# Output scatters through disjoint views, token splits one slot apart, and a reordered first joint in an attention, expert and dense kernel

## Chip, cores and metric

The kernel runs on one core of a Trainium2 chip. The metric is the device time of that core in microseconds (us), the median of three runs.

## What is computed

The reference is a chain of three parts. Attention runs over 4 batches, 8 heads, 576 positions and 64 values per head; four heads see a window of 32 positions, four a dilated one (every fourth of 128). Its output is a matrix of 2304 tokens by 512. Then comes a mixture of 8 experts in which each token goes to one expert alone, and last a dense layer over all tokens:

```python
e_idx = argmax(x @ w_gate + modality_bias[modality_id])
for e in range(8):                       
    out[e_idx == e] = gate_w * (relu(x[e_idx == e] @ w1[e]) @ w2[e])
...
h = x @ w_in                             
g = where(h >= 1, h, where(h <= -1, 0, (h + 1) ** 2 / 4))
return g @ w_out
```

The expert layers are 512 to 1024 to 512, the dense ones 512 to 2048 to 512. All of it is fp32 with the accuracy kept by splitting each operand into a high part and a low part (the rest) in a rounded format: a product is three matmuls, high by high, low by high and high by low.

## The kernel before

The engines are TensorE (PE, whose weight loads are shown as PEld), VectorE (DVE), ScalarE (ACT), GpSimd (POOL) and SyncE (SP, which issues most transfers). Each engine works off its instructions in the order in which the program records them, since the scheduling is manual; an engine that waits holds up all that is queued behind it. So the order of the calls in the code is the order on each engine.

**Attention and routing** come first. The attention output is gated and written to memory, and the routing (class `Route`) counts on DVE which token goes where; its results are registers that the engines load from a tile `ri` (`load_regs`, L570, through `values`, L560).

**The experts** run as steps 0 to 15, each a chunk of 256 tokens of one expert. `gather` (L592) collects the token rows by indirect DMA on POOL, in two halves of 128; `scale` (L620, DVE) or `scale_act` (L616, ACT) multiplies them by the gate; `tx` (L627) transposes them on PE into a bank and splits them into `xh` (ACT) and `xl` (DVE). `half_a` (L777) runs the first expert layer, eight output tiles `fb` of `l1_wide`; `half_b` (L803) the second, four output tiles `d` of `l2_wide`. Between the tiles stand pieces of other work: `work` yields parts of the weight conversion; `small_x`, `small_1`, `small_h`, `small_2`, `small_y`, `small_out` handle a remainder of up to 32 tokens and stand under a branch on the register `sm` (L667); `resplit` (L885) splits an expert's weights again, under a branch on the register `c` (L887); `load_w` under one on `ld`. Step 0 and step 1 overlap with the routing and are special: `first` (L733) is step 0's second half, `small_ids` and the register loads stand in step 1's `half_a`, and `positions` behind it computes where each token lies. Steps 9 to 15 stand under nested branches on the number of chunks that the routing counted; for this input they are not taken, though the rows for step 9 are gathered, scaled and transposed in steps 6 to 8, as the rows of any next step.

**The dense part** (`dense`, L1340) takes the tokens in three groups g of 768 and the 2048 hidden columns in eight pairs of blocks, so 24 pairs n. A pair's first product is a 2x2 block product in the manner of Strassen, with seven products instead of eight: the seven slots j of a pair (`SLOTS`, L1480). A slot's matmuls go to bank X or Y, and `part` keeps three of the partial products (copies on ACT, L1501) until `joined` (L1413, DVE) adds them. Each finished block goes through `relu` (ACT: relu and square, L1395 and L1396), `square` (DVE: the clamp of L1403, then ACT's cast to the high part, L1404) and, a slot later, `lows` (DVE: the low part, L1411). The second product (`l2_tile`, L1422) sums six banks po[0] to po[5] over the eight pairs of a group; `flow` puts one or two of its tiles into each slot, always those of the pair before. The first pair has no seven products but four plain blocks, in banks po[5], po[4], po[3] and Y (L1464).

Two further streams of work stand in the slots. The tokens of the next group are summed (`y_sum`, raw sums T1 to T4) and split (`y_split`, L1371): a cast to the high part on ACT, and right behind it the low part on DVE; the list `late` says in which slot. And the weights of the next pair are split (`split_in`, `split_out`, one piece per `next`) in the first eight pairs, after which they come back from a cache in memory. When the last pair of a group has finished a bank, `send` (L1430) copies it on ACT and scatters its 128 rows of 512 values to the output by an indirect DMA on POOL (L1435), 18 in all, six per group. All 18 write the same tensor `out`, and each waits for the one before.

## Time and profile before

| | |
|---|---|
| runs | 802.9, 804.3, 804.7 us |
| median of the runs | 804.32 us |
| the profiled execution's own time | 804.42 us |
| its span in the profile | 802.5 us |
| TensorE busy | 746.1 us, 93% of the span |
| weight loads / DVE / ACT / POOL busy | 661.5 / 506.7 / 379.3 / 98.5 us |
| mean granted clock of TensorE, full being 1 | 0.982 |

How to read it: the span runs from the first to the last instruction of one profiled execution, and all times in it count from the span's start. An engine that is busy for most of the span is not thereby the bound of every stretch, so the table of stretches shows busy time and the granted clock for windows of 25 us. The list of waits names, for an engine and a line, what its last semaphore came from, with the total in us, how many times and the longest. In the timeline a row in square brackets shows how long its engine had stood idle and what ended that. "ACTq" or "PEq" is the engine's sequencer, which also does register loads and branches.

### The profile page before, as it was taken

The page shows a single profiled execution, that of the slowest core. Times are in us where ns is not written, and L with a number is a line of the kernel's source. Part 1 is how long each engine was busy: PE and PEld are TensorE (multiplying, and loading weights), DVE is VectorE, ACT ScalarE, POOL GpSimd, SP SyncE. Part 2 cuts the span into 40 slices and gives each one's busy share as a digit, 9 for nine tenths or more (in the row PEclk, how much of TensorE's full clock was granted, in tenths as well). Part 3 has the DMA queues.
Part 4 walks back from the last instruction along what each step waited for, and adds up shares of the span by engine and source line. Part 5 has one row for each costly group of instructions (what it writes and reads, how often), then busy time and mean ns, then how long its engine had stood idle before and what let it go on. Part 6 is the DMA issues. An engine that isn't in the chain of part 4 may idle for free. (4 is left out here: it accounts for less than half of the span.)

```text
span 802.5 us, 15304 instructions
## 1 busy us (share of the span) xinstructions
PE 746.1 (93%) x5545; PEld 661.5 (82%) x5547; DVE 506.7 (63%) x1217; ACT 379.3 (47%) x948; POOL 98.5 (12%) x101
## 2 busy tenths in 40 slices
PE   7998879789999999999879999899999999999991
PEld 4887769788998999889868898788889878889980
DVE  4789886684677888784677777754454454433430
ACT  3667643213323323532457666675354566444550
POOL 3335542120100001000000000001000002000002
PEclk9999989999999999999999999999999999999996
DMA  7779751277989968713429766387446435653411
GB/s 196 205 224 288 237 166 42 55 245 242 327 274 318 339 185 269 271 59 105 125 103 339 290 250 223 151 295 278 156 170 229 178 145 205 257 193 145 146 64 65
DMA packets 66345, 161.55 MB, mean 201 GB/s; under 512 B 8448, under 2 KB 25856, under 8 KB 60240
## 3 DMA queue, kind: packets, MB, share of 16 engines
q1 hardware_dynamic: 62592, 148.58, 54.5%
q0 software_dynamic: 3520, 11.55, 4.3%
q8 instruction: 48, 0.79, 0.4%
q14 instruction: 41, 0.34, 0.1%
q10 hardware_dynamic: 144, 0.29, 0.1%
HBM read 119.36 MB, written 41.04 MB: 200 GB/s over the span
## 5 line engine op out<-in xcount | busy, mean ns | idle before, releaser
L1403 DVE SCALAR_TENSOR_TENSOR t<-x,t 128x384 f32<-128x384 f32 x92 | 51.3, 558 | 76.7 <-ACT t L1396 76.6
L1426 PE MATMUL d_o<-d_ob,gh 128*128 128x512 f32 x288 | 90.5, 395 | 0.0
L1426 PE MATMUL d_o<-d_plain,gh 128*128 128x512 f32 x288 | 89.6, 392 | 0.0
L643 PE MATMUL ps_e<-hh,whi 128*128 128x256 f32 x288 | 82.7, 287 | 0.4
L643 PE MATMUL ps_e<-hl,whi 128*128 128x256 f32 x288 | 81.1, 282 | 0.0
L643 PE MATMUL ps_e<-hh,wlo 128*128 128x256 f32 x288 | 81.0, 281 | 0.0
L1395 ACT ACTIVATE t<-x 128x384 f32<-128x384 f32 x92 | 48.3, 525 | 54.2 <-DVE x L1416 54.2
L1404 ACT CAST gh<-t 128x384 fp32r<-128x384 f32 x96 | 49.4, 515 | 44.6 <-DVE t L1403 44.3
L1411 DVE TENSOR_TENSOR gl<-t,gh 128x384 fp32r<-128x384 f32 x96 | 53.2, 554 | 17.8 <-ACT gh L1404 15.5
L1176 ACT ACTIVATE p<-ps_s,nb 128x96 f32<-128x96 f32 x144 | 47.1, 346 | 33.2 <-DVE su L1184 32.3
L1426 PEld LDWEIGHTS d_o<-d_ob,gh 128*128 128x128 f32 x288 | 53.4, 190 | 5.8
L1426 PEld LDWEIGHTS d_o<-d_plain,gh 128*128 128x128 f32 x288 | 53.0, 188 | 6.1
L1426 PE MATMUL d_o<-d_ob,gl 128*128 128x512 f32 x144 | 57.4, 399 | 0.0
L1426 PE MATMUL d_o<-d_plain,gl 128*128 128x512 f32 x144 | 57.1, 396 | 0.0
L1416 DVE TENSOR_TENSOR x<-d_y,d_u 128x384 f32<-128x384 f32 x46 | 25.5, 554 | 48.7 <-ACT d_u L1501 48.7
L643 PEld LDWEIGHTS ps_e<-hh,whi 128*128 128x128 f32 x288 | 54.5, 189 | 1.0 <-issue 1.0
L643 PEld LDWEIGHTS ps_e<-hh,wlo 128*128 128x128 f32 x288 | 54.5, 189 | 0.0
L643 PEld LDWEIGHTS ps_e<-hl,whi 128*128 128x128 f32 x288 | 54.4, 189 | 0.0
L1396 ACT ACTIVATE t<-t 128x384 f32<-128x384 f32 x96 | 50.5, 526 | 3.0
L1501 ACT COPY d_u<-d_x 128x384 f32<-128x384 f32 x46 | 22.0, 478 | 61.7 <-PE d_x L1383 61.7
L1435 POOL DMA_INDIRECT out<-o,pid x18 | 17.6, 975 | 267.5 <-ACT o L1434 198.1
L643 PE MATMUL ps_s<-xh,whi 128*128 128x256 f32 x152 | 45.6, 300 | 5.0 <-DVE hl L654 3.2
(439 smaller groups left out, 1902.9 us busy)
## 6 DMA issues: line engine op xcount, KB each, us to landing
raw<-in_w SPq DMA_DIRECT2D x48, 512.0 KB
d_ab<-cache SPq DMA_DIRECT2D x15, 1024.0 KB
d_ab<-cache SPq DMA_DIRECT2D x15, 768.0 KB
r<-in_w_in SPq DMA_DIRECT2D x16, 512.0 KB
r<-in_w_out SPq DMA_DIRECT2D x16, 512.0 KB
wsc<-cva SPq DMA_DIRECT2D x32, 256.0 KB
cache<-d_ab SPq DMA_DIRECT2D x8, 1024.0 KB
d_ob<-cache SPq DMA_DIRECT2D x8, 1024.0 KB
```

The costliest lines, as they stand in the source:

```text
L643: self.tc.nc.tensor.matmul(ps, a, b, start=(i == 0 and j == 0), stop=(i == n - 1 and j == 2))
L1176: nc.scalar.activation(p[:, j, :], s[:, j, :], ACTF.Exp, scale=scale, bias=nb[:, j:j + 1], accum_out=su[:, j:j + 1])
L1395: nc.scalar.activation(b.t, x, ACTF.Relu, scale=0.5, bias=0.5)
L1396: nc.scalar.activation(b.t, b.t, ACTF.Square)
L1403: nc.vector.scalar_tensor_tensor(b.t, x, 1.0, b.t, op0=ALU.max, op1=ALU.min)
L1404: nc.scalar.copy(b.h, b.t)
L1411: nc.vector.tensor_tensor(b.l, b.t, b.h.bitcast(F32), op=sub)
L1416: nc.vector.tensor_tensor(x, bank, other, op=add)
L1426: nc.tensor.matmul(po[i], a[:, q], o[:, x, f, :], start=(first and j == 0), stop=(last and j == 2))
L1435: nc.gpsimd.indirect_dma_start(out=out[:, :], out_offset=bass.IndirectOffsetOnAxis(ap=pid[:, n:n + 1], axis=0), in_=t, in_offset=None)
L1501: nc.scalar.copy(part[("p1", "u2", "u3")[j // 2]], bank)
```

## The change

It has five parts, all in the order or the place of work; no arithmetic changes.

1. Each scatter writes through its own view of the output, of 18 that are declared disjoint.
2. In step 0's second half, `scale_act(1)` comes ahead of the third tile, and half of the re-split ahead of the fourth; the other half goes into step 1. In step 1 the load of the nine `sm` registers on PE and ACT becomes one of four before the seventh tile of the first layer and one of five before the second tile of the second layer; the small pieces, the routing's `positions` and the transposes for step 2 move later.
3. What steps 7 and 8 did for steps 9, 10 and 11 (scaling, transposes, a gather) stands in the branch of step 9.
4. The first dense pair's blocks go to X, Y, po[5] and po[4], and T2 and T1 are split in its third and fourth block's place.
5. `y_split` is cut into `y_high` (the cast) at the end of a slot and `y_low` (the subtraction) behind the `lows` of the next; the second sums T3 and T4 come a slot earlier, output weights' split a slot later, and `split_in` has one pause more.

```diff
                 late = rt.late_counts()
             next(late)
         for d in range(HP):
+            if d == 2:
+                self.scale_act(1)
             self.l2_wide(d, slice(0, 256))
             if d == 0:
                 rt.late_ids(self.b.A[0])
...
                 rt.more_ids(self.b.A[1])
                 next(regs)
             if d == 2:
-                self.scale_act(1)
                 self.tx(1, 0)
                 self.tx(1, 1)
-        self.resplit(1, 0, 8)
+                self.resplit(1, 0, 4)
         next(regs)
         next(regs)
         return regs
...
                 self.w.load(i, self.regs[s]["ne"])
     def half_a(self, s, wide, work, rt=None):
-        at = {5: self.small_x, 6: self.small_1, 7: self.small_h} if s == 1 else {0: self.small_x, 2: self.small_1, 4: self.small_h}
+        at = {7: self.small_x} if s == 1 else {0: self.small_x, 2: self.small_1, 4: self.small_h}
         for fb in range(8):
             if s == 1 and fb == 2:
                 self.small_ids(rt, work)
             if s == 1 and fb == 6:
                 self.scale(2)
-            if s == 1 and fb == 4:
-                self.load_regs("sm", R_SM, 1, 10, [ENG.PE, ENG.Activation])
+            if s == 1 and fb == 6:
+                self.load_regs("sm", R_SM, 1, 5, [ENG.PE, ENG.Activation])
                 self.scale3(1)
             if s > 1 and fb in (2, 4, 6):
                 self.resplit(s, fb, fb + 2)
...
                 self.small(s, at[fb])
                 if at[fb] == self.small_h:
                     self.sum_h()
+            if s == 1 and fb == 1:
+                self.resplit(1, 4, 8)
             if wide:
                 self.l1_wide(fb)
                 if s > 1 or fb > 1:
                     next(work, None)
                     next(work, None)
-            if fb == (7 if s == 1 else 3):
+            if s > 1 and fb == 3:
                 self.load_w(s, 0, 4)
+        if s == 1:
+            self.small(s, self.small_1)
+            self.load_w(s, 0, 4)
         for _ in work:
             pass
-    def half_b(self, s, wide, work):
-        self.small(s, self.small_2)
-        self.load_w(s, 4, 8)
-        if wide:
-            self.tx(s + 1, 0)
-            self.tx(s + 1, 1)
+    def half_b(self, s, wide, work, rt=None):
+        late = s == 1
         off = bass.ds(self.regs[s]["off"], 256)
         for d in range(HP):
-            if d == 2:
+            if late and d == 1:
+                self.load_regs("sm", R_SM, 5, 10, [ENG.PE, ENG.Activation])
+                self.small(s, self.small_h)
+                self.sum_h()
+                rt.positions()
+            if d == (3 if late else 0):
+                self.small(s, self.small_2)
+                self.load_w(s, 4, 8)
+            if wide and s != 8 and d == (2 if late else 0):
+                self.tx(s + 1, 0)
+                self.tx(s + 1, 1)
+            if not late and d == 2:
                 self.small(s, self.small_y)
                 if s > 0:
                     self.sum_y()
-            if d == 3:
+            if not late and d == 3:
                 self.small(s, self.small_out)
             if wide:
                 self.l2_wide(d, off)
...
             if d == 2:
                 self.scale3(s + 1)
                 self.resplit(s + 1, 0, 2)
+        if late:
+            self.small(s, self.small_y)
+            self.sum_y()
+            self.small(s, self.small_out)
         for _ in work:
             pass
...
             self.load_sp(9, NS)
             self.load_mode(10, NS)
             self.load_off(9, NS)
+            self.scale(9)
+            self.scale(10)
+            self.tx(9, 0)
+            self.tx(9, 1)
+            self.gather(11)
         n = CV_STEPS[s] if cv else (0, 0)
         parts = cv.start(n[0]) if n[0] else []
         self.either(s, lambda wide: self.half_a(s, wide, cv.work(parts, True, s < 7) if cv else self.ahead(s, 0, regs), rt))
...
         self.gather3(s + 1)
         if s == CV_LAST + 1:
             self.m2.load_in()
-        if rt:
-            rt.positions()
         if cv:
             cv.loads()
         more = cv.start(n[1]) if n[1] else []
-        self.either(s, lambda wide: self.half_b(s, wide, cv.work(more, False, s < 7) if cv else self.ahead(s, 1)))
-        self.gather(s + 3)
-        self.scale(s + 2)
+        self.either(s, lambda wide: self.half_b(s, wide, cv.work(more, False, s < 7) if cv else self.ahead(s, 1), rt))
+        if s != 8:
+            self.gather(s + 3)
+        if s not in (7, 8):
+            self.scale(s + 2)
         if cv:
             cv.loads()
...
         V.tensor_tensor(a21, a11, a21, op=ALU.subtract)
         V.tensor_tensor(a11, a22, a11, op=ALU.subtract)
         V.tensor_tensor(a12, a12, a11, op=ALU.subtract)
+        yield
         yield
         x = t.rearrange("p f (a k) -> p (f a) k", a=2)
         S.copy(s[:, 0], x)
...
         tp = st.enter_context(tc.tile_pool(name="d_t", bufs=3))
         ps = st.enter_context(tc.tile_pool(name="d_ps", bufs=1, space=PSUM))
         op = st.enter_context(tc.tile_pool(name="d_out", bufs=6))
+        outs = dram_disjoint_views(out, NT)
         m2.more(yp)
         X, Y = (ps.tile([128, 512], F32, name=f"d_{c}")[:, 0:G2] for c in "xy")
         po = [ps.tile([128, 512], F32, name=f"d_o{i}") for i in range(6)]
...
             for c in range(2):
                 nc.vector.tensor_tensor(raw[k][c], src(g, a, c), raw[b][c] if b in raw else src(g, b, c), op=sub)
-        def y_split(g, k, c, b=None, vec=False):
+        def y_high(g, k, c, b=None, vec=False):
             h, l = yt[k][c]
             b = DIRECT.get(k, b)
             x = raw[k][c] if b is None else src(g, b, c)
             (nc.vector.tensor_copy if vec else nc.scalar.copy)(h, x)
-            nc.vector.tensor_tensor(l, x, h.bitcast(F32), op=sub)
+            y_lows.append((h, l, x))
+
+        def y_low():
+            while y_lows:
+                h, l, x = y_lows.pop(0)
+                nc.vector.tensor_tensor(l, x, h.bitcast(F32), op=sub)
+
+        def y_split(*a, **k):
+            y_high(*a, **k)
+            y_low()
+
+        y_lows = []
         def mm(bank, lst, start, stop):
             n = len(lst)
...
                 t = op.tile([128, 512], F32, tag="o", name="o")
                 nc.scalar.copy(t, p)
                 nc.gpsimd.indirect_dma_start(
-                    out=out[:, :], out_offset=bass.IndirectOffsetOnAxis(ap=pid[:, n:n + 1], axis=0), in_=t, in_offset=None)
+                    out=outs[n][:, :], out_offset=bass.IndirectOffsetOnAxis(ap=pid[:, n:n + 1], axis=0), in_=t, in_offset=None)
         def queue(n, blk):
             m = n % NP
...
         for i, (t, f) in enumerate(((0, 0), (0, 1), (1, 1), (1, 0))):
             k1, k2 = (("B11", "B21"), ("T3", "B22"))[t]
             w = m2.plain[:, :, f, :]
-            bank = (po[5], po[4], po[3], Y)[i][:, 0:G2]
+            bank = (X, Y, po[5], po[4])[i][:, 0:G2]
             mm(bank, [(w, c, yt[k1][c]) for c in range(2)] + [(w, 2 + c, yt[k2][c]) for c in range(2)], True, True)
             if i == 0:
                 for k in ("T3", "B22"):
...
             if i < 2:
                 next(w_out)
                 y_sum(0, f"T{i + 1}")
+                if i == 1:
+                    for c in range(2):
+                        y_high(0, "T2", c)
             else:
-                y_split(0, "T2", i - 2)
+                y_low()
+                if i == 2:
+                    for c in range(2):
+                        y_high(0, "T1", c)
         queue(0, blk)
-        late = [(7, 0, "T1"), (9, 0, "T3"), (10, 0, "T4")]
+        late = [(8, 0, "T3"), (9, 0, "T4")]
         SLOTS = (("B11", 0, 0), ("B21", 0, 1), ("T2", 1, 0), ("T1", 1, 3), ("T3", 1, 2), ("T4", 0, 2), ("B22", 1, 1))
         for n in range(1, NPAIR):
             g, m = divmod(n, NP)
...
                 flow((0, 1, 1, 1, 2, 1, 0)[j] if last else (2, 2, 2, 1, 2, 1, 2)[j])
                 if j in (0, 2, 4):
                     nc.scalar.copy(part[("p1", "u2", "u3")[j // 2]], bank)
-                if late and late[0][0] <= 7 * n + j:
-                    _, h, k2 = late.pop(0)
-                    for c in range(2):
-                        y_split(h, k2, c)
                 lows(square())
+                y_low()
                 if j == 1:
                     blk[0, 0] = joined(Y, part["p1"])
                 if j == 4:
...
                     blk[1, 0] = joined(X, part["u3"])
                 if j == 6:
                     blk[0, 1] = joined(Y, part["u2"])
+                if late and late[0][0] <= 7 * n + j:
+                    _, h, k2 = late.pop(0)
+                    for c in range(2):
+                        y_high(h, k2, c)
                 next(prep, None)
-                if j in (2, 3):
+                if j in (3, 4):
                     next(w_out, None)
                 send()
                 if m == NP - 1 and not last:
                     late.append((7 * n + j + 1, g + 1, k))
-                if n == 1 and j in (1, 2):
-                    y_sum(0, f"T{j + 2}")
+                if n == 1 and j in (0, 1):
+                    y_sum(0, f"T{j + 3}")
                 if j == 5 and g < 2 and 2 <= m < 6:
                     y_sum(g + 1, f"T{m - 1}")
             if n <= NP:
```

The order shows three places. First POOL at the end of the program, the six scatters of the last token group (`out` is the output, `o` the copied tile, `pid` the row numbers; in brackets stand the semaphores waited for, DMASW those of POOL's transfers, eight in turn, Activation that of the ACT copy). Before:

```order
L1435 DMA out<-o,pid 2304x512 [waits DMASW7_49,Activation_49]
L1435 DMA out<-o,pid 2304x512 [waits DMASW0_49,Activation_49]
L1435 DMA out<-o,pid 2304x512 [waits DMASW1_49,Activation_49]
L1435 DMA out<-o,pid 2304x512 [waits DMASW2_49,Activation_49]
L1435 DMA out<-o,pid 2304x512 [waits DMASW3_49,Activation_49]
L1435 DMA out<-o,pid 2304x512 [waits DMASW4_49,Activation_49]
```

and now:

```order
L1471 DMA out<-o,pid 2304x512 [waits DMASW3_49,Activation_49]
L1471 DMA out<-o,pid 2304x512 [waits DMASW4_49,Activation_49]
L1471 DMA out<-o,pid 2304x512 [waits DMASW5_49,Activation_49]
L1471 DMA out<-o,pid 2304x512 [waits DMASW6_49,Activation_49]
L1471 DMA out<-o,pid 2304x512 [waits DMASW7_49,Activation_49]
L1471 DMA out<-o,pid 2304x512 [waits DMASW0_49,Activation_49]
```

The form of the rows is the same in both; before, the DMASW semaphore is that of the scatter just ahead, and now it is that of the scatter eight places ahead, which used the same semaphore.

The second place is PE in step 1, around the register load (`ri` holds the registers, `ps_s`, `ps_e` are banks, `xh` and `xl` the tokens' parts, `hh` and `hl` the hidden values' parts, `whi` and `wlo` the weights' parts). Before, in the first layer:

```order
L643 MATMUL ps_e_2038<-xl,whi_97 128x256
L604 UNCONDITIONAL_BRANCH
L561 TENSOR_LOAD ri
L613 COMPARE_AND_BRANCH
L613 UNCONDITIONAL_BRANCH x2
L773 UNCONDITIONAL_BRANCH
L643 MATMUL ps_s_81<-xh,whi_98 128x256
L643 MATMUL ps_s_81<-xh,wlo_106 128x256
```

and now, later in the first layer,

```order
L644 MATMUL ps_s_82<-xl,whi_99 128x256
L562 TENSOR_LOAD ri
L614 COMPARE_AND_BRANCH
L614 UNCONDITIONAL_BRANCH x2
L644 MATMUL ps_e_2037<-xh,whi_98 128x256
L644 MATMUL ps_e_2037<-xh,wlo_106 128x256
```

and once more in the second layer:

```order
L644 MATMUL ps_e_2039<-hl_2056,whi_103 128x256
L562 TENSOR_LOAD ri
L668 COMPARE_AND_BRANCH
L695 MATMUL ps_r<-cs,hs 128x128 x4
L695 MATMUL ps_s_83<-cs,hs 128x128 x4
```

One load has become two, each behind a whole tile's matmuls, and each followed by a branch.

The third place is DVE in the first dense pair, from its second or third block on (`d_rT` are raw sums, `d_T20h` and the like the high part of T2's half 0, `t`, `gh`, `gl` a block's value and its two parts; the first operand of the clamp L1403, or now L1439, is the bank). Before:

```order
L1403 SCALAR_TENSOR_TENSOR t<-d_o_7883,t 128x384
L1411 TENSOR_TENSOR gl<-t,gh 128x384
L1376 TENSOR_TENSOR d_T20l<-d_rT_7918,d_T20h 128x384
L1403 SCALAR_TENSOR_TENSOR t<-d_o_7882,t 128x384
L1411 TENSOR_TENSOR gl<-t,gh 128x384
L1376 TENSOR_TENSOR d_T21l<-d_rT_7919,d_T21h 128x384
L1376 TENSOR_TENSOR d_T10l<-d_rT_7916,d_T10h 128x384
L1376 TENSOR_TENSOR d_T11l<-d_rT_7917,d_T11h 128x384
L1403 SCALAR_TENSOR_TENSOR t<-d_y,t 128x384
L1411 TENSOR_TENSOR gl<-t,gh 128x384 x2
```

and now:

```order
L1439 SCALAR_TENSOR_TENSOR t<-d_y,t 128x384
L1447 TENSOR_TENSOR gl<-t,gh 128x384
L1406 TENSOR_TENSOR d_T20l<-d_rT_7921,d_T20h 128x384
L1406 TENSOR_TENSOR d_T21l<-d_rT_7922,d_T21h 128x384
L1439 SCALAR_TENSOR_TENSOR t<-d_o_7887,t 128x384
L1447 TENSOR_TENSOR gl<-t,gh 128x384
L1406 TENSOR_TENSOR d_T10l<-d_rT_7919,d_T10h 128x384
L1406 TENSOR_TENSOR d_T11l<-d_rT_7920,d_T11h 128x384
L1439 SCALAR_TENSOR_TENSOR t<-d_o_7886,t 128x384
L1447 TENSOR_TENSOR gl<-t,gh 128x384
```

The low parts of T2 and T1 now stand in pairs behind a block's clamp and low part, and the last bank cleared in the pair is one of `d_o`; `d_y` is cleared two blocks earlier.

## Rows read from the trace of the kernel before

**Rows 1.** The page: busy time of the engines.

```profile
PE 746.1 (93%) x5545; PEld 661.5 (82%) x5547; DVE 506.7 (63%) x1217; ACT 379.3 (47%) x948; POOL 98.5 (12%) x101
```

**Rows 2.** Table by stretches; columns: window, length, busy us (instructions) by engine, clock, DMA.

```profile
150.00:175.00 25.00, 20.33 (x164) 19.09 (x163) 18.10 (x77) 3.96 (x11) 4.71 (x5) 0.93 0.34 108
200.00:225.00 25.00, 25.00 (x212) 22.47 (x204) 17.18 (x37) 8.42 (x19) 2.79 (x3) 1.00 0.87 291
400.00:425.00 25.00, 19.85 (x92) 17.32 (x91) 17.59 (x34) 14.90 (x30) 0.00 (x0) 0.93 0.34 127
475.00:500.00 25.00, 25.00 (x126) 22.42 (x125) 19.41 (x36) 15.55 (x28) 0.00 (x0) 1.00 0.63 238
```

**Rows 3.** Waits of PE, whole span; columns: total us, times, longest.

```profile
PE d_x L1383 <- ACT d_u L1501: 2.9, 2, 1.5
PE d_y L1383 <- DVE x L1416: 2.9, 3, 1.3
PE d_o L1383 <- ACT d_B210h L1375: 2.4, 1, 2.4
...
PE ps_r L634 <- ACT xgb L618: 1.7, 1, 1.7
...
PE d_x L1383 <- DVE x L1416: 1.2, 2, 0.8
...
PE ps_s L643 <- ACTq L887: 0.5, 1, 0.5
```

**Rows 4.** Timeline of the tail; columns: start us, duration us, engine, line, operation, tiles.

```profile
778.44 0.59 ACT L1434 COPY o<-d_o 128x512 f32<-128x512 f32 x1 [1.53 <-PE d_o L1426]
...
779.30 0.97 POOL L1435 DMA_INDIRECT out<-o,pid  x1 [92.34 <-ACT o L1434]
...
784.81 0.39 PE L1426 MATMUL d_o<-d_plain,gl 128*128 128x512 f32 x1
785.24 0.59 ACT L1434 COPY o<-d_o 128x512 f32<-128x512 f32 x1 [0.77 <-PE d_o L1426]
...
796.78 0.97 POOL L1435 DMA_INDIRECT out<-o,pid  x1 [2.52 <-DMA out<-o,pid]
```

**Rows 5.** The scatters' line L1435 in the tail, 776 to 804: issue to landing.

```profile
DMA to landing us min/median/max: 2.7/2.7/2.7
```

**Rows 6.** The gathers' line L597 138 to 150; ns, first and last start.

```profile
L597 POOL DMA_INDIRECT xgb<-x_dram,ids x2: 957/1118/1278, 140.3 to 141.9; - x2
L597 POOL DMA_INDIRECT xga<-x_dram,ids x2: 957/957/957, 143.1 to 144.4; - x2
...
DMA to landing us min/median/max: 4.0/4.3/4.7
```

**Rows 7.** Timeline of step 1 around the register load.

```profile
158.73 0.17 DVE L474 CAST ri<-rt_sm 1x17 int32<-1x17 f32 x1
...
161.70 0.39 PE L643 MATMUL ps_s<-xh,whi 128*128 128x256 f32 x1 [3.20 <-DVE hl L654]
```

**Rows 8.** The register loads' line L561, whole span; ns min/median/max.

```profile
L561 POOLq TENSOR_LOAD <-ri x2: 638/1453/2268, 158.9 to 317.1; - x2
...
L561 PEldq TENSOR_LOAD <-ri x1: 2362/2362/2362, 158.9 to 158.9; - x1
```

**Rows 9.** Timeline of step 8: the transposes of step nine's tokens.

```profile
374.22 0.63 PE L634 MATMUL ps_r<-cs,xgb 128*128 128x128 f32 x4 [0.30 <-DVE hl L654]
```

**Rows 10.** Timeline of the first two dense pairs.

```profile
405.28 0.56 DVE L1376 TENSOR_TENSOR d_T21l<-d_rT,d_T21h 128x384 fp32r<-128x384 f32 x1 [1.46 <-ACT d_T21h L1375]
...
407.01 0.55 DVE L1403 SCALAR_TENSOR_TENSOR t<-d_y,t 128x384 f32<-128x384 f32 x1
...
407.62 0.61 PE L1383 MATMUL d_y<-d_B210h,d_ab 128*128 128x384 f32 x2 [3.70 <-DVE t L1403]
...
411.71 0.52 PE L1383 MATMUL d_x<-d_T20h,d_ab 128*128 128x384 f32 x2
```

**Rows 11.** Timeline of the first change of token groups: DVE.

```profile
519.62 0.56 DVE L1376 TENSOR_TENSOR d_T30l<-d_rT,d_T30h 128x384 fp32r<-128x384 f32 x1 [0.42 <-ACT d_T30h L1375]
```

More of the change, by code (lines that the diff above doesn't have):

```diff
@@ L8 @@
 from concourse._compat import with_exitstack
+from concourse.ap import dram_disjoint_views
 F32 = mybir.dt.float32
```

## Prediction, written before the changed kernel was run

> **What bounds the kernel now.** I read the page's engine line first: TensorE (PE) is busy 746.1 of 802.5 us [rows 1], so work taken off another engine counts only where PE, or the end of the program, waits for it. Then the table by stretches: in 200 to 225 and in 475 to 500 PE is busy 25.00 of 25 us at the full clock, so in most of the mixture of experts and in most of the dense part the matmuls themselves are the time, while in 150 to 175 and in 400 to 425 PE is busy about 20 of 25 and the granted clock is 0.93 [rows 2]. A mean of 0.93 in 25 us is about 3.5 us at the lower of the two levels (1.2 GHz, otherwise 2.4), and half of that, 1.75 us, is lost. Third, PE's list of waits: these are what the change can take [rows 3]. Fourth, the timeline of the tail: PE's last matmul starts at 784.81 and takes 0.39, yet the span ends at 802.5 [rows 4]. So 17 us at the end belong to the output.
>
> The profiled execution took 804.4 us, its span 802.5, so 1.9 lie outside; the median of the runs is 804.3. The sum below goes against 804.4. About 0.2%, 1.6 us, is what a measurement of this kernel can tell from no change.
>
> **1. The scatters.** Their number and bytes stay; what goes is a wait. The last output copy on ACT starts at 785.24 and takes 0.59, but the sixth scatter of the tail starts at 796.78, having sat 2.52 idle for the landing of the scatter before it [rows 4]; in the tail a scatter lands 2.7 after it starts [rows 5]. In the new order the six wait for their ACT copy and for a scatter eight earlier, which is long done. The first scatter started at 779.30, 0.27 after its copy ended at 779.03 [rows 4]; by the same step the last would start at 785.83 + 0.27 = 786.1, a gain of 796.78 - 786.1 = 10.7. One scatter issues in 0.97, and copies end 1.36 apart ((785.24 - 778.44) / 5), so POOL keeps up. What the trace doesn't show is several scatters in flight: before, each lands alone, 2.7 after it starts. The nearest rows are four gathers that start 1.3 to 1.6 apart and land 4.0 to 4.7 after their starts [rows 6]. If the last scatter took their longest, 4.7 in place of 2.7, 2.0 of the gain would go. Gain 8.7 to 10.7; I take 10.5, near the upper end, since the scatters read ready tiles and in the tail nothing else uses the DMA engines. The scatters of the other two token groups end in mid-program beside PE's work and give nothing.
>
> **2. Steps 0 and 1 of the experts.** Four edits. (a) Scaling the step's second token half on ACT comes before the third output tile: PE waited 1.7 for it [rows 3]; the bounds are 0 and 1.7. Its two gathers start at 140.3 and 141.9 and land 4.0 to 4.7 later [rows 6], by 145.0 and 146.6: the first half can be scaled earlier, the second hardly. I take 0.7, under half of the wait. (b) The branch tests of the weight re-split stand in two places rather than in one lump: PE waited 0.5 for ACT's tests there [rows 3]; I take 0.5. (c) The load of nine register values on PE's and ACT's sequencers becomes a load of four, two output tiles later, and one of five, in the second half of the step. PE's load began at 158.90, when the cast that writes its values ended [rows 7], and took 2.362 [rows 8]; with the branches behind it PE stood still for 3.20 up to 161.70 [rows 7], and the low clock came right after: 1.75 more. From 158.90 + 2.36 = 161.26 to 161.70 are 0.44 of branch tests; the 0.4 before the load is its wait for the cast, which the later place takes away. What four and five cost no row shows. POOL's load of two took 0.638, PE's of nine 2.362 [rows 8]: a straight line gives 0.246 per value, 1.13 and 1.38 us. With 0.44 of branches behind each, the two stalls make 3.4 against 3.2 + 1.75 = 4.95: gain 1.6, if the clock stays up, which the shorter idle times of 1.7 and 2.4 [rows 3] speak for, since the low clock was seen only behind the 3.20 and the 3.7. If it falls once more, -0.2; if PE's queued matmuls cover both loads, 4.95. The Trainium skill (Runtime: NRT & Kernel Launch, section Instruction fetch mechanics) gives about 200 ns per register for such a load; by it the two loads would be 0.8 and 1.0 and the gain 2.3. The row of nine, 0.262 per value, is above that, and I go by the row. (d) The small remainder pieces and their sums move later; their branches aren't taken in this step, so only tests move. The routing positions on DVE move into the second half, ahead of the low part of the next step's tokens: DVE is busy 18.10 of 25 there [rows 2], so I cost this at nothing; without that cover the next step's first matmuls wait, at most for a piece of some us. Sum 0.7 + 0.5 + 1.6 = 2.8, from 0.3 (0, 0.5 and -0.2) to 7.2. The steps behind are bound by PE [rows 2], so it passes through.
>
> **3. Step nine's rows.** Here step 9 isn't taken, so all that moves into its branch goes: on PE eight transposes, two groups of 0.63 with 0.30 idle ahead [rows 9]: 0.3 + 2 x 0.5 = 1.3 (the groups overlap). Their ACT and DVE work, two scalings and a pair of gathers lie beside PE's work. PE's wait of 2.4 for the first dense cast [rows 3] hangs on the jump over steps 9 to 15, and I leave it. Gain 1.3, from 1.0 to 2.2, the upper end if DVE arrives at the jump earlier.
>
> **4. The first dense pair.** Its four blocks go to X, Y, po5, po4 instead of po5, po4, po3, Y. Before, Y was held by the fourth block: DVE stood behind the cast of T2 for 1.46 and cleared Y only at 407.01 + 0.55, and PE waited 3.70 up to 407.62 [rows 10] and then ran at half clock, 1.75. In the new order Y belongs to the second block, cleared two blocks earlier. Without the stall slot 1 of pair 1 begins at 407.62 - 3.70 = 403.9; a pair has 42 matmuls of the first product and 36 of the second in 7 slots, so a slot takes 25 us / 126 x 78 / 7 = 2.2 us [rows 2], so slot 2 begins at 406.1 and not at 411.71 [rows 10]: 5.6, and I take the 5.5 of the two terms. What is late next is the fourth block in po4, wanted by an output tile of slot 2 at about 407; it clears at about 407.0 + 0.55 less DVE's wait of 1.46, at 406.1. Of the 1.4 that PE waited later in that pair (2.9 less 1.5 [rows 3]) I take 0.5. Gain 6.0, from 3.7 (the wait goes, the low clock comes from another) to 6.9.
>
> **5. Token splits.** Between groups PE waits 2.9 for the ACT copies of the partial products (1.4 of it is pair 1's, above), 2.9 and 1.2 for DVE's joining sums [rows 3]: 7.0 less 1.4 = 5.6 in two transitions. The reason is DVE's order: the low part of a split stands right behind its cast on ACT, so DVE idles for it, 0.42 in one slot [rows 11], and the sums that clear the banks come after. Now the cast is issued at the end of a slot and the subtraction a slot later, behind the blocks' own. The work itself remains, and in the first transition the weights' splits beside it. So I take 4.2 of the 5.6, from 2.8, half, to 5.6. The extra pause in the split of the input weights, and the output weights a slot later, cost nothing while they are ready a pair ahead: in 475 to 500 DVE is busy 19.41 and ACT 15.55 of 25 [rows 2].
>
> **Sum.** 10.5 + 2.8 + 1.3 + 6.0 + 4.2 = 24.8: 804.4 - 24.8 = 779.6, forecast **779.6**. The least of all terms together, 8.7 + 0.3 + 1.0 + 3.7 + 2.8 = 16.5, gives 788; the most, 10.7 + 7.2 + 2.2 + 6.9 + 5.6 = 32.6, gives 772.
>
> **Rivals.** *The scatters still run one after another*, in the queue rather than at the semaphore: the first lands at 779.3 + 2.7 = 782.0, the sixth 5 x 2.7 later at 795.5 and not at 796.78 + 2.7 = 799.5, a gain of 4.0 in place of 10.5: 786.1; with no gain at all, 790.1. For it: the wait removed was for a landing. Against it: by that rule the fourth gather, started 4.1 after the first, would land some 6.7 after its start, and the longest took 4.7 [rows 6]. The Trainium skill (DMA: Bandwidth & Descriptors, section Two DMAs through the same engine are not ordered) says that descriptors of a queue start in order but are pipelined. The gathers agree with that. Chance 0.08.
>
> *The dense start's stall only moves*: ACT comes late with T2 or T1 and PE stands in slot 2 long enough for the clock to fall again; of the 6.0 some 1.0 is left: 784.6. DVE busy 17.59 and ACT 14.90 of 25 there [rows 2] speak against it, the strict order on each engine for it. Chance 0.12.
>
> *Slower*: the extra pause makes the weights of a pair late. Seven pairs split weights; if PE then waits a slot in each, 2.2, and the clock falls behind each, 1.75, that is 27.7 against 24.8: 807.3. It decides only where the wait comes near the 3.2 behind which the low clock was seen; without the fall it costs 15.4 and leaves 795. For it: the sums of DVE stand behind casts of ACT everywhere in this part. Against: PE has no wait at all in 475 to 500, and the weights are used a pair later. Chance 0.03, and 0.02 for no change.
>
> **How the numbers follow.** Forecast as it stands, within its terms, 0.75. All cases but the slower one lie at or below 790, so the range is 771 to 790: the sum's most with a little room, since its terms were read from a profile by hand, and at the other end its least and the queue's rival. The chances left out are those of slower and of no change, and some of a time under 771; faster 0.95, same 0.02, slower 0.03.
>
> **What would show it.** Scatters in the tail 1.36 apart, with the ACT copy as their releaser, and a span that ends some 17 - 10.5 = 6.6 us behind PE's last matmul; two register loads on PE of 1.1 to 1.4 and the clock at 1.00 where 150 to 175 had 0.93; no transposes in step 8; no wait of Y in pair 1 and the clock up; PE's waits at the two transitions under 1.5 together. A serial queue would show landings that grow from scatter to scatter; a moved stall would show PE waiting for ACT's casts, or a DVE sum, in pair 1; a new wait in pairs 2 to 8 on the input weights would make the forecast wrong.

## Result and the profile after

The changed kernel takes 775.18 us in the median of four runs (773.65 to 778.05), the kernel before 803.78 in the runs beside it: a ratio of 0.965, 95% interval 0.962 to 0.968. The forecast was 779.6, the range 771 to 790.

The profiled execution has a span of 772.4 us against 802.5. The page's busy line shows that PE does hardly less, and stands idle for a smaller share (answers to [rows 1]):

```profile
PE 742.0 (96%) x5539; PEld 660.1 (85%) x5539; DVE 501.6 (65%) x1211; ACT 376.5 (49%) x946; POOL 99.3 (13%) x99
```

The table by stretches, columns as in [rows 2]; the dense part begins some 6 us earlier than before, so its windows lie earlier too:

```profile
150.00:175.00 25.00, 23.21 (x203) 22.44 (x202) 19.58 (x73) 5.89 (x14) 6.92 (x5) 1.00 0.43 132
375.00:400.00 25.00, 22.66 (x130) 21.39 (x131) 17.75 (x35) 14.72 (x32) 0.00 (x0) 0.93 0.43 150
400.00:425.00 25.00, 25.00 (x126) 22.43 (x125) 20.96 (x41) 17.12 (x34) 0.00 (x0) 1.00 0.59 214
500.00:525.00 25.00, 24.98 (x124) 21.93 (x123) 17.54 (x33) 18.80 (x40) 5.26 (x7) 1.00 0.72 256
```

The clock no longer falls in 150 to 175. It falls in 375 to 400 instead, where the dense part begins, and nowhere in 400 to 425. PE's longest waits behind the attention (answers to [rows 3]) are these. All those on `d_u`, on `x` and on Y are gone. The one on `hs`, in step 2, is new, and so are the two on PE's sequencer (PEq), 0.58 and 0.91, in step 1; the one on L707 stands in the kernel before too, with the same 1.7:

```profile
PE d_x L1419 <- ACT d_B210h L1400: 2.3, 1, 2.3
...
PE ps_r L695 <- ACT hs L684: 1.7, 1, 1.7
PE ps_s L707 <- issue: 1.7, 1, 1.7
...
PE ps_e L644 <- PEq L668: 1.5, 2, 0.9
```

The tail (answers to [rows 4]): the scatters start 1.36 apart with the ACT copy as their releaser, and the last starts 0.27 after its copy has ended. The span ends 6.5 behind PE's last matmul, where it was 17.3.

```profile
760.04 0.97 POOL L1471 DMA_INDIRECT out<-o,pid  x1 [107.23 <-ACT o L1470]
...
761.40 0.97 POOL L1471 DMA_INDIRECT out<-o,pid  x1 [0.39 <-ACT o L1470]
...
765.55 0.39 PE L1462 MATMUL d_o<-d_plain,gl 128*128 128x512 f32 x1
765.97 0.59 ACT L1470 COPY o<-d_o 128x512 f32<-128x512 f32 x1 [0.77 <-PE d_o L1462]
766.83 0.97 POOL L1471 DMA_INDIRECT out<-o,pid  x1 [0.38 <-ACT o L1470]
```

Where the rest came from is read at the first matmul of a pair. In the timelines of before and then after, the rows are the first matmuls of pairs 1, 2, 7, 8 and 9. A pair that waits for nothing takes 15.68.

```profile
401.33 0.51 PE L1383 MATMUL d_x<-d_B110h,d_ab 128*128 128x384 f32 x2
...
424.25 0.51 PE L1383 MATMUL d_x<-d_B110h,d_ab 128*128 128x384 f32 x2
...
502.68 0.51 PE L1383 MATMUL d_x<-d_B110h,d_ab 128*128 128x384 f32 x2
...
521.64 0.62 PE L1383 MATMUL d_x<-d_B110h,d_ab 128*128 128x384 f32 x2 [0.80 <-DVE x L1416]
...
539.14 0.51 PE L1383 MATMUL d_x<-d_B110h,d_ab 128*128 128x384 f32 x2
```

```profile
396.20 0.51 PE L1419 MATMUL d_x<-d_B110h,d_ab 128*128 128x384 f32 x2
...
411.88 0.51 PE L1419 MATMUL d_x<-d_B110h,d_ab 128*128 128x384 f32 x2
...
490.32 0.51 PE L1419 MATMUL d_x<-d_B110h,d_ab 128*128 128x384 f32 x2
...
506.00 0.51 PE L1419 MATMUL d_x<-d_B110h,d_ab 128*128 128x384 f32 x2
...
522.10 0.51 PE L1419 MATMUL d_x<-d_B110h,d_ab 128*128 128x384 f32 x2
```

Pair 1 takes 15.68 instead of 22.92, pair 7 15.68 instead of 18.96, pair 8 16.10 instead of 17.50. Pairs 15 and 16 take 15.68 and 15.92 instead of 16.30 and 17.52. So the two profiles differ by stretches like this (a matmul or a wait with the same place in both as the mark, PE throughout):

| stretch | forecast | measured |
|---|---|---|
| attention, up to the routing's counts (118.73 against 117.28) | 0 | 1.45 |
| routing and steps 0 to 5, of which 2 to 5 differ only by the new wait (to a mark in step 6, 309.58 against 304.31) | 2.8 | 3.82 |
| steps 6 to 8 and step nine's rows (to the first dense matmul, 392.69 against 386.36) | 1.3 | 1.06 |
| first dense pair, 8.64 against 9.84, and pair 1 | 6.0 | -1.20 + 7.24 = 6.04 |
| changes of token groups: 3.28 + 1.40 + 0.62 + 1.60 | 4.2 | 6.90 |
| tail, 17.3 against 6.5 | 10.5 | 10.84 |
| sum | 24.8 | 30.1 |

The attention's code is the same. In all fourteen profiles, these two and the twelve below, that mark lies between 116.6 and 119.3 whatever was changed, and the changed kernel itself has 117.28 here and 118.25 in a second profile, so the 1.45 is within chance. The sum of the table, 30.1, is that of two single profiles; the medians differ by 28.6.

### The profile page after: what moved, and what is told of

The parts are those of the page before. It is cut to its first block, busy times and chain, and to the rows that moved or that the text cites. A ratio compares the mean times of both kernels' runs of the same rounds, so it can differ in the third digit from the quotient of the medians.

```text
span 772.4 us, 15270 instructions
## 1 busy us (share of the span) xinstructions
PE 742.0 (96%) x5539; PEld 660.1 (85%) x5539; DVE 501.6 (65%) x1211; ACT 376.5 (49%) x946; POOL 99.3 (13%) x99
## 5 line engine op out<-in xcount | busy, mean ns | idle before, releaser
L1439 DVE SCALAR_TENSOR_TENSOR t<-x,t 128x384 f32<-128x384 f32 x92 | 51.4, 558 | 80.0 <-ACT t L1432 79.8
L663 ACT COPY xy<-ps_e 128x256 f32 (+1 forms) x36 | 13.4, 373 | 79.6 <-PE ps_e L644 65.2
```

The source lines that it names most:

```text
L1439: nc.vector.scalar_tensor_tensor(b.t, x, 1.0, b.t, op0=ALU.max, op1=ALU.min)
```

## Experiments

These runs start from the changed kernel and differ from it by the edit shown; `views_only` alone starts from the kernel before. Times are medians, ratios go against the kernel before, which had 803.2 to 804.0 beside them, and the changed kernel's 775.18 is from the first set of runs.

**no_views** and **views_only**: the views alone taken out, or (the same lines the other way round, with the views' declaration) put in. Long lines are cut at the dots.

```diff
-                    out=outs[n][:, :], out_offset=...
+                    out=out[:, :], out_offset=...
```

> The changed kernel with all 18 scatters writing the one output tensor again. Theory of the semaphore (each scatter waited for the landing of the one before): the tail's scatters stand 3.49 us apart again, the span ends some 17 us behind the last matmul, and the time is 775.2 + 10.8 = 786. Rival (the tail got shorter because the order of the last tiles changed, or for another reason): it stays within 2 us of 775.

> The kernel before with the disjoint views alone. Theory that the parts add up: 803.8 - 10.8 = 793.0, six scatters 1.36 us apart in the tail, last matmul at 785 as before. Rival (the scatters of the first two token groups had also held something up, or several in flight disturb the weight transfers in mid-program): last matmul moved by more than 1.5 us, and the time outside 791.5 to 794.5.

no_views took 785.69, ratio 0.979 (0.977 to 0.981); views_only 792.58, ratio 0.987 (0.984 to 0.989). The timeline of no_views has its scatters 3.49 apart behind the landing again, and the span ends 17.1 behind PE's last matmul:

```profile
773.90 0.97 POOL L1471 DMA_INDIRECT out<-o,pid  x1 [2.52 <-DMA out<-o,pid]
777.40 0.97 POOL L1471 DMA_INDIRECT out<-o,pid  x1 [2.52 <-DMA out<-o,pid]
```

So the scatters are worth 10.5 in one direction and 10.9 in the other, and the semaphore was the cause. In views_only PE ended at 784.70 against 785.2, but that says little: its first dense matmul came 2.35 earlier than before (390.34 against 392.69) and its first two dense pairs took 1.85 longer, mostly since its clock fell at other places. What shows that the twelve scatters in mid-program disturbed nothing is that pairs 2 to 22 took what they had taken before, each within 0.02. Beside the weights' transfers these scatters land up to 8.8 after their starts, and up to 8.2 in no_views, where one waits for the other; in the tail it is 2.7 to 2.8 in either, as before.

**old_banks**, **old_first_splits** and **old_pair**: the first dense pair's two edits undone, one at a time and together.

```diff
-            bank = (X, Y, po[5], po[4])[i][:, 0:G2]
+            bank = (po[5], po[4], po[3], Y)[i][:, 0:G2]
...
-                if i == 1:
-                    for c in range(2):
-                        y_high(0, "T2", c)
             else:
-                y_low()
-                if i == 2:
-                    for c in range(2):
-                        y_high(0, "T1", c)
+                y_split(0, "T2", i - 2)
         queue(0, blk)
-        late = [(8, 0, "T3"), (9, 0, "T4")]
+        late = [(7, 0, "T1"), (8, 0, "T3"), (9, 0, "T4")]
```

> The changed kernel with the first pair's four blocks in po5, po4, po3 and Y as before; the splits of T2 and T1 stay in their new places. Theory of the banks, as the prediction had it (Y held by the fourth block): PE waits over 3 us for Y in pair 1 again, 775.2 + 5 to 6 = 781. Rival, the order of the splits on ACT and DVE: by the changed kernel's timeline the fourth block is cleared at 399.05 and Y is wanted at 398.63, so the wait is about 0.5 and the time 775.7.

> The changed kernel with its new banks, but in the first pair T2's halves are split each behind its own block, cast and low part together, as before, and T1's in the first slot of pair 1. Theory of the banks: Y is free early, no wait of PE over 1 us in pair 1, the time within 1 of 775.2. Rival, the order of the splits: DVE stands behind ACT's casts as before, PE waits some 1 to 2 us in pair 1 for po4 or for X, and the time is 776 to 779.

> The changed kernel with both edits of the first dense pair undone: blocks in po5, po4, po3 and Y, and T2's halves split behind their blocks, T1's in pair 1. With only one of them undone no wait over 0.3 was left in pair 1. Theory that either edit alone lifts the wait for Y: here it is back, 2.8 to 3.7 us, pair 1 takes 20 to 22 us instead of 15.68, and the time is 775.5 + 4 to 6 = 779.5 to 781.5. Rival (the wait was lifted by a third thing, the split weights' pieces that come a slot later): no wait over 1 us here either, 776 to 777.

Times 776.11, 776.73 and 777.46 (ratios 0.967 each, within 0.965 to 0.970). The medians lie too near to chance to decide, so the timeline does. With the old banks alone, pair 1 (first row to second) takes 15.68 and waits for nothing:

```profile
397.81 0.51 PE L1419 MATMUL d_x<-d_B110h,d_ab 128*128 128x384 f32 x2
...
413.49 0.51 PE L1419 MATMUL d_x<-d_B110h,d_ab 128*128 128x384 f32 x2
```

The fourth block's clamp ends at 399.85 there, and Y is taken at 400.24. With the old splits alone pair 1 takes 17.46. It has no wait for Y either. PE stands a little at a time, longest by the list for `d_u` ahead of T3, 0.24, and for T4's low part, 0.28:

```profile
411.29 0.44 PE L1419 MATMUL d_x<-d_T40l,d_ab 128*128 128x384 f32 x1 [0.28 <-DVE d_T40l L1406]
```

With both, pair 1 takes 17.95, and the wait for Y is back, released by the clamp of the fourth block:

```profile
401.28 0.61 PE L1419 MATMUL d_y<-d_B210h,d_ab 128*128 128x384 f32 x2 [1.98 <-DVE t L1439]
```

So each of the two edits lifts the wait for Y by itself. The order of the splits is worth 1.8 on the new banks and 2.3 on the old ones; the banks are worth 0.5 with the old order and nothing with the new one, so by pair 1 the changed kernel could have kept its old banks. For old_pair I had expected a wait of 2.8 to 3.7 and a pair of 20 to 22; it came back with 1.98 and 17.95, which is 2.3 of pair 1's 7.24. The kernel before also had T1's low parts ahead of the fourth block's clamp, and the splits of T3 and T4 in one piece: that is the next edit.

**whole_splits**: cast and subtraction in one piece and ahead of the blocks' steps again, and the sums and splits of T3 and T4 a slot later.

```diff
-        late = [(8, 0, "T3"), (9, 0, "T4")]
+        late = [(9, 0, "T3"), (10, 0, "T4")]
...
+                if late and late[0][0] <= 7 * n + j:
+                    _, h, k2 = late.pop(0)
+                    for c in range(2):
+                        y_split(h, k2, c)
                 lows(square())
-                y_low()
...
-                if late and late[0][0] <= 7 * n + j:
-                    _, h, k2 = late.pop(0)
-                    for c in range(2):
-                        y_high(h, k2, c)
...
-                if n == 1 and j in (0, 1):
-                    y_sum(0, f"T{j + 3}")
+                if n == 1 and j in (1, 2):
+                    y_sum(0, f"T{j + 2}")
```

> The changed kernel with a token split in one piece again, cast and subtraction one behind the other ahead of the blocks' own steps, as before; T3 and T4 of the first group a slot later. The weights' pauses and the first pair stay. Theory (DVE's idle time behind the casts made the transitions wait): PE waits at pairs 7, 8, 15 and 16 again, 6.9 us longer in all, and up to 1.4 in pair 1: 775.2 + 7 to 8.3 = 782 to 783.5. Rival (the extra pause in the input weights' split or the output weights a slot later did it): within 1.5 of 775.2.

782.46, ratio 0.974 (0.972 to 0.977): 7.3 slower. PE's list of waits has the three of [rows 3] back, 6.9 in all:

```profile
PE d_y L1419 <- DVE x L1452: 2.6, 2, 1.3
...
PE d_x L1419 <- DVE x L1452: 2.2, 2, 1.7
PE d_x L1419 <- ACT d_u L1543: 2.1, 2, 1.5
```

Pairs 1, 7, 8, 15 and 16 take 17.40, 18.74, 17.50, 16.30 and 17.51. The 1.7 in pair 1 is not Y's: it is the old wait for `d_u` at T4, 1.45, while Y stays free. The weights' extra pause and the later output weights stayed in this run, so they are not what helped. Which of the cut in two, the place behind the blocks' own steps and the earlier sums did it, no run separates.

**old_joint**: `first`, `half_a` and `half_b` in the order of before, `positions` ahead of `half_b`.

```diff
-            if s == 1 and fb == 6:
-                self.load_regs("sm", R_SM, 1, 5, [ENG.PE, ENG.Activation])
+            if s == 1 and fb == 4:
+                self.load_regs("sm", R_SM, 1, 10, [ENG.PE, ENG.Activation])
...
-            if late and d == 1:
-                self.load_regs("sm", R_SM, 5, 10, [ENG.PE, ENG.Activation])
...
```

> The changed kernel with steps 0 and 1 in the order of before (one register load of nine, scaling and re-split in their old places, the routing positions ahead of the second half). Theory: PE's waits of 1.7, 0.5 and 3.2 and the low clock behind the last come back and the wait of 1.74 in step 2 goes: 775.2 + 3.8 = 779.0. The 1.5 us that the changed kernel's profile was ahead of the other before step 0 are then chance, and the span up to the routing is as long in this run as in either. Rival (they came from this part): 775.2 + 5.3 = 780.5, with the attention 1.5 longer.

778.24, ratio 0.969 (0.967 to 0.971): 3.1 slower, and the waits are those of before (0.5 not shown), with no wait for `hs`:

```profile
PE ps_s L644 <- DVE hl L655: 3.2, 1, 3.2
...
PE ps_r L635 <- ACT xgb L619: 1.6, 1, 1.6
```

The clock falls behind the 3.20, as before. From the attention's mark to that in step 6 it takes 190.5, before 190.85, the changed kernel 187.03. The attention is 118.48 long here, within the spread above, so nothing says that its 1.45 came from this part. The four edits were undone together; what each is worth is read from profiles alone.

**rows_nine**: step nine's scaling, transposes and gather in steps 7 and 8.

```diff
-            if wide and s != 8 and d == (2 if late else 0):
+            if wide and d == (2 if late else 0):
...
-            self.scale(9)
-            self.scale(10)
-            self.tx(9, 0)
-            self.tx(9, 1)
-            self.gather(11)
...
-        if s != 8:
-            self.gather(s + 3)
-        if s not in (7, 8):
-            self.scale(s + 2)
+        self.gather(s + 3)
+        self.scale(s + 2)
```

> The changed kernel with step nine's scaling, transposes and gather in steps 7 and 8 again. Theory: PE does eight transposes more, 1.0 to 1.3: 776.2 to 776.5. Rival (the jump over the steps not taken begins earlier because DVE is done earlier): up to 2 us.

775.85, ratio 0.965 (0.963 to 0.968): 0.7 more, less than the runs tell apart. In the timelines the way from the last branch of step 8 to the first dense matmul is 24.78 against 23.72, so step nine's rows cost 1.1 there: eight transposes 0.11 apart and 0.30 of idle time ahead of them.

**load_earlier**, then once more beside the unaltered kernel as **changed_again** and **earlier_again**. The new wait in step 2 has a chain of its own. In the changed kernel SP issues the eight weight loads of step 1 over 12.62 us, four of them behind `small_2`, which reads the same tiles and was moved to the last output tile. The first load of the weight conversion is issued next, ACT waits 5.80 for its landing, and the copy that PE wants stands behind that on ACT:

```profile
163.20 12.62 SPq L193 DMA_DIRECT2D raw<-in_w  x8
176.79 0.38 SPq L937 DMA_DIRECT2D r<-in_w_in  x1
...
185.03 0.66 ACT L960 ACTIVATE cva<-r 128x512 f32<-128x512 f32 x1 [5.80 <-DMA r<-in_w_in]
...
186.84 0.55 PE L695 MATMUL ps_r<-cs,hs 128*128 128x128 f32 x3 [1.74 <-ACT hs L684]
```

```diff
-            if d == (3 if late else 0):
+            if d == (2 if late else 0):
                 self.small(s, self.small_2)
                 self.load_w(s, 4, 8)
```

> The changed kernel with step 1's second weight load, and the piece of the remainder in front of it, one output tile earlier. Theory of the new wait in step 2 (the loads for the conversion stand behind the eight weight loads on SP, which this change made four of late, so ACT stood 5.8 us for the first of them and PE 1.74 behind it): the weight loads are issued some 2.9 us earlier, PE's 1.74 goes or shrinks under 0.5, 775.2 - 1.5 = 773.7. Rival (the transfers themselves are the bound there, not their issue): PE still waits over 1.2 in step 2, and the time is the same.

> The changed kernel once more, unaltered, beside the next two on one chip: 775.5 within 1.5. Its profile shows the wait of 1.5 to 2.3 for the remainder's hidden values in step 2; whether the low clock falls on the first dense matmuls is open, as eight profiles with an idle time of 2.3 to 2.5 there show both.

> The changed kernel with step 1's second weight load one output tile earlier, once more, on the same chip. Theory: no wait in step 2, 1.5 to 2.5 below the changed kernel in the row above it. Rival (its 772.76 was a lucky set of runs): within 0.7 of the changed kernel.

load_earlier took 772.76, ratio 0.962 (0.960 to 0.964). In the second set changed_again took 774.94 (0.964, 0.962 to 0.966), with the wait for `hs` again (1.81), and earlier_again 772.60 (0.961, 0.959 to 0.963). The gain of 2.3 to 2.4 came out twice, though the intervals overlap a little. In earlier_again the weight loads are issued over 10.70, ACT waits 2.66, and PE's matmul row has no wait:

```profile
162.97 10.70 SPq L193 DMA_DIRECT2D raw<-in_w  x8
176.58 0.38 SPq L937 DMA_DIRECT2D r<-in_w_in  x1
...
181.67 0.66 ACT L960 ACTIVATE cva<-r 128x512 f32<-128x512 f32 x1 [2.66 <-DMA r<-in_w_in]
...
184.72 0.49 PE L695 MATMUL ps_r<-cs,hs 128*128 128x128 f32 x3
```

This version beats both kernels. The expected gain came, but not by the conversion's load being issued earlier: that is at 176.79 in one kernel and at 176.58 in the other. What got shorter is its way from issue to use, 8.2 against 5.1 us. The DMA engines are full ahead of it in both, busy for 0.99 and 0.97 of 174 to 185, but from 171 to 174 their share is 0.53 in the changed kernel and 1.06 in this one (packets are counted where they start), whose second four weight loads go out from 168.63 on instead of 172.69. So the transfers were the bound, as the rival had it, though the time did not stay the same: an earlier issue of the weights helped, by this reading because it filled idle time of the DMA engines.

**earlier_warm**: the same with 22 filling matmuls ahead of the jump.

```diff
-            for _ in range(14):
+            for _ in range(22):
                 tc.nc.tensor.matmul(self.b.X[0], ...)
```

> The same with 22 instead of 14 filling matmuls of PE ahead of the jump over steps 9 to 15. Theory: the eight more fill about 1.9 of the 2.4 us in which PE stands idle before the first dense block, which still begins when ACT's casts arrive; so the clock never falls there, and the time is that of the row above or up to 1.2 less. Rival: the jump on PE begins only when the filling matmuls are done, and the entry is 1.9 later, 774.7.

773.06, ratio 0.961 (0.959 to 0.963), the same. PE's idle time before the first dense block fell from 2.30 to 1.52 only, and that block began 1.0 later after step 8 (24.71 against 23.67). So some of the filling delayed the entry, as the rival had it, though by 1.0 and not 1.9. The clock stayed up, but it did so without the filling in load_earlier and earlier_again too, so this run doesn't show what the filling does for it.

## Why the prediction was right, and where its terms were not

**1, the scatters**: 10.5 forecast, 10.84 in the profile, 10.5 and 10.9 in the two experiments. The upper bound was the right one: the last scatter starts 5.6 before the span's end, and before it was 5.7, so with several in flight the last lands no later in the tail. The serial queue is ruled out: in the tail of views_only each of the six lands 2.7 to 2.8 after its start.

**2, steps 0 and 1**: 2.8 forecast, 3.8 measured in the first pair of profiles, and the terms were off both ways. Of (a) and (b), PE's waits of 1.7 and 0.5 became 0.45 and none in this profile. In changed_again (a)'s wait was 1.84 again: the second gather's rows could be used 5.3 after its start there and 3.9 here, so (a) hangs on the gathers, as the lower bound of 0 had it. In (c) the loads were sized well, 1.13 and 1.38 forecast and 1.19 and 1.25 measured, but I let both stop PE:

```profile
L562 PEldq TENSOR_LOAD <-ri x2: 1186/1217/1248, 155.5 to 163.9; - x2
...
165.64 0.36 PE L644 MATMUL ps_e<-hh,whi 128*128 128x256 f32 x1 [0.91 <-PEq L668]
```

The first ran from 155.5 to 156.7 while PE went on with the matmuls recorded ahead of it, without a gap until 158.9. Only the second cost something, 0.91. The old load began at 158.90, when the cast that it waited for ended [rows 7], and PE had run out of matmuls at 158.50. So by these two profiles (c) gave about 4.0, namely 3.20 + 1.75 - 0.91, and not 1.6; the case "PE's queued matmuls cover both loads" was half true. The Trainium skill (Runtime: NRT & Kernel Launch, section Instruction fetch mechanics) has about 200 ns per register, a figure for registers loaded from HBM. Here four and five values from the tile `ri` took 0.30 and 0.25 each, so the measured line was the better price. In (d) "only tests move" was wrong. The branch tests cost PE 0.58 and 0.46 in their new places, against 0.37 and 0.30 in the old ones. And the step's second weight load is taken, it moved with `small_2`, and I did not follow its transfers: 1.74 of new wait.

The 3.8 is also a matter of which profiles are compared. From the attention's mark to step 6, the order of before takes 190.85 and 190.51 (old_joint) where the clock falls behind the register load, and 188.69 in views_only, where it doesn't. The new order takes 186.8 to 187.1 in six profiles, 188.48 in changed_again with its late gather, and 189.01 in old_banks, where the clock fell behind the wait for `hs`, 2.31 long that time. So between two single executions this part gives anything from nothing to 4.0; in the medians it gives 3.1.

**3, step nine's rows**: 1.3 forecast, 1.06 measured.

**4, the first dense pair**: the size came out (6.0 against 6.04) by luck. The 6.0 were 5.5 for Y's wait with its low clock, and 0.5 of the 1.4 that PE waited later in the pair. That later wait went whole, and whole_splits brings 1.73 for it back; the 5.5 are what is left of pair 1's 7.24. Against both stands 1.20 that the forecast had at nothing: the clock fell at the entry. The term mis-sized is thus "of the 1.4 ... I take 0.5". The mechanism was half of it. With the new banks Y is free early, as the prediction has it (old_first_splits), but with the old ones it is free in time as well once DVE no longer stands behind T2's casts (old_banks), and without the new order of the splits the new banks leave pair 1 at 17.46. old_pair brings 2.3 of the 5.5 back; the rest should be a longer wait for Y, behind T1's low parts, and the low clock after it. That needs old_pair and whole_splits in one kernel, which wasn't tried. The rival of a moved stall was right for the clock alone: it fell with no stall in slot 2.

**5, token splits**: 4.2 forecast, 6.9 measured, the largest error. I took three quarters of the listed waits, since the work remained; that share was mis-sized, for none of them was left. And a wait costs more than the list says: the six waits of pairs 7, 8, 15 and 16 add up to 5.58, the pairs were 6.90 longer. About 0.2 more goes with each. At the first of them, at 515.79, the matmul behind the wait starts together with its own weight load and takes 0.45, where the next ones, whose weights come ahead, take 0.33 to 0.34.

Of the 5.3 by which the profiles differ more than forecast, 2.7 are the token splits, 1.45 the attention, 1.0 steps 0 and 1. The rest of the way to the medians has no mechanism: single runs of one kernel differ by up to 4.4. The rival of slower, late weights, shows nowhere: pairs 2 to 6 take 15.68 to 15.69.

## What to carry to other kernels

Writes to disjoint rows of one tensor wait for each other as long as the program cannot see that they are disjoint; where such writes end the program, declaring views lets them follow each other as fast as their data come. Here that was every 1.36 instead of every 3.49, so 2.1 for each of six but the first. In engines that work in order, try the second half of a two-engine step (cast on one, subtraction on the other) a slot later and behind the blocks' own steps, rather than right behind the first half, and look at that order before changing banks. When a step is moved, follow its transfers as well: four weight loads that were issued three output tiles later here held up another load's landing, with it an engine and then PE.

## What the runs showed of the hardware

The granted clock does not follow from the length of the idle time alone. PE stood idle for 2.30 to 2.45 before the first dense block in thirteen profiles. In eight of them, the changed kernel's among them, the lower level (1.2 of 2.4 GHz) came on that block, which then took 3.0 to 3.8 instead of 2.4; in five it did not. The same program shows both: for changed_again the stretch that had 0.93 above reads

```profile
375.00:400.00 25.00, 22.55 (x142) 20.94 (x141) 16.06 (x31) 13.77 (x30) 0.00 (x0) 1.00 0.44 148
```

And in views_only the old register load's idle time of 3.22, which I had priced with 1.75 of low clock, left the clock at 1.00:

```profile
150.00:175.00 25.00, 20.52 (x177) 19.38 (x176) 19.44 (x76) 4.81 (x12) 4.80 (x5) 1.00 0.43 133
```

The prediction had it that the low clock was seen only behind the 3.20 and the 3.7, and let 1.7 and 2.4 speak for a clock that stays up. That was misread already in the profile of the kernel before, where it also came, in the attention, behind 2.11:

```profile
75.00:100.00 25.00, 20.66 (x305) 17.13 (x305) 22.37 (x72) 16.21 (x70) 13.63 (x10) 0.93 0.82 250
...
77.13 1.27 PE L1193 MATMUL ps_t<-cs,p 128*96 128x128 f32 x5 [2.11 <-DVE pt L1195]
```

So 1.2 to 1.75 us of this kernel's time at each such gap are chance, and a forecast should carry them as a range rather than as part of the wait's price.
